# Moving the addition of the softmax's small constant from VectorE to GpSimd, one step ahead of the reciprocal

## The chip, the cores and the metric

The kernel runs on one core of a Trainium2 chip. The metric is the device time of one execution in microseconds (us). The kernel before takes 601.28 us, the median of three runs (601.18 to 601.39).

## What is computed

Banded attention with eight global keys, then two gated products. In the reference, cut to what matters here:

```python
def _attn_ref(q, k, v, n_global, n_local):
    ...
    scores = scale * np.matmul(q, k.transpose(0, 1, 3, 2))
    ...
    scores = scores + bias[None, :, :, :]
    scores = np.where(keep, scores, -1000000000.0)
    scores = scores - np.max(scores, axis=-1, keepdims=True)
    a = np.exp(scores)
    a = a / (np.sum(a, axis=-1, keepdims=True) + 1e-09)
    return np.matmul(a, v).astype(np.float32)
```

There are 2 batches, 8 heads, 768 positions and 64 numbers to a head; a query sees 96 keys up to its own and the first 8. What attention gives, 1536 x 512, goes through `(a * b) @ w3 @ w_out` with `a = x @ w1` and `b = x @ w2`, and then through a second product of that kind. The change touches the row sums of the softmax: the constant that is added to them, 1e-9, and the reciprocal that is taken of them.

## The kernel before

Attention works on tiles of 128 queries against 256 keys (their own 128 and the 128 before; the first tile of a batch sees 128). There are 12 tiles, and each has 4 units of two heads: 48 units `u`. `band_attention` is a software pipeline: each turn of its loop, called a step here, issues one stage each of several units, and since the instructions are put into the engines' queues in the order of the calls, and every queue is worked off in order, the order of the calls is the order on each engine. The next instruction of a queue waits until all that it needs is done, and holds those behind it.

In step `u`:

- TensorE gets the scores of units `u` and `u+1` in every second step (`band_scores`, L410 and L427).
- ScalarE gets the two exponentials of unit `u-2` (`band_exp`, L456), each of which also gives a row sum in one of the two columns of `z` (the rows with READ_ACCUMULATOR in the trace).
- `band_turn` transposes a unit four or five steps behind on TensorE (L480) and copies it on ScalarE (L482); `band_values` multiplies by the values (L516).
- VectorE gets `band_max` of unit `u-1`: two instructions L444, one for each head, which add the bias to the scores and find the row extreme.
- `band_norm` of unit `u-3`: VectorE adds the constant to `z` (L465), takes the reciprocal (L467), and GpSimd multiplies the exponentials by it, one instruction for each head (L469).
- In some steps the following come as well: splitting the next tile's keys and queries (ScalarE L368 and GpSimd L369 in one step, VectorE L380 and L383 in the next), the copy of the global keys L394, storing the result (ScalarE L491, VectorE L498), and the conversion of weights (ScalarE L89, L90, L115; VectorE L94, L98, L102, L119).

The stages written as generators are collected in `turns`, and `feed` takes them round robin: the first piece of each, then the second piece of each. So before the change VectorE's order in a step is: first L444, L465, the pieces of the other stages up to their first `yield`, second L444, L467, the rest. A stage without a `yield` (such as `band_high` with L369) runs at once when it is called, ahead of all pieces of the generators.

Between the steps, `next(filler)` puts matrix products of the next layer (`gate`, L669 to L671, with L677 on ScalarE and L678 on VectorE) into the queues. How much of it a step takes is counted in the code (`spent`) and doesn't depend on times.

Of the kernel before, what the change touches and what calls it, by code (L numbers as in the profile page):

```python
# [14 lines left out]
ALU = mybir.AluOpType  # L15
# [6 lines left out]
EPS = 1.0e-9  # L22
# [9 lines left out]
class Emitter:  # L32
# [418 lines left out]
    def band_exp(self, u):  # L451
# [7 lines left out]
            )  # L459
        self.sm[u] = (s, z, lo)  # L460

    def band_norm(self, u):
        nc = self.nc
        s, z, lo = self.sm[u]
        nc.vector.tensor_scalar_add(z, z, EPS)  # L465
        yield
        nc.vector.reciprocal(z, z)  # L467
        for j in range(2):
            nc.gpsimd.tensor_scalar(  # L469
                out=s[:, j, lo:], in0=s[:, j, lo:], scalar1=z[:, j : j + 1], scalar2=1.0, op0=ALU.mult, op1=ALU.mult  # L470
            )
# [51 lines left out]
    def band_attention(self, filler):  # L523

        self.v, self.qs, self.sp, self.sm, self.pt, self.pv = ({} for _ in range(6))
        self.kq = dict(enumerate(self.kq01))
        self.ks = self.const.tile([P, 3, self.H, P], F32R, name=self.name("ks"))
        self.globs = self.const.tile([P, self.H, MAX_GLOBAL], F32, name=self.name("globs"))
        C = self.C
        nt = self.B * self.NB  # L530
        nu = nt * C
        self.patient = True
        masks = self.band_masks()
        self.feed_load(1, self.nc.scalar)
        next(masks)

        self.nc.vector.tensor_copy(out=self.nf, in_=self.ni.bitcast(U32))
        next(masks)
        block_stages = (
            (0, self.band_load_v), (C - 1, self.band_global), (-3, self.band_low), (-4, self.band_high), (-6, self.band_load),  # L540
        )
        early = sorted((C * t + lag, t, n) for t in range(nt) for n, (lag, _) in enumerate(block_stages) if C * t + lag < 0)
        for _, t, n in early:
            if t and n != len(block_stages) - 1:
                for _ in block_stages[n][1](t) or ():
                    pass
        spent = 0.0
        turned = valued = 0
        stores = {}
        u = -1  # L550
        while self.stored < nt:
            u += 1
            self.step = u
            at = lambda lag, stage: stage(u - lag) if 0 <= u - lag < nu else None
            at(0, self.band_scores)
            at(2, self.band_exp)
            while turned < min(nu, u - 4 if u < 16 else u - 5):
                self.band_turn(turned)
                turned += 1


            while valued < min(nu, u - 5 if u < 16 else u - 6) and (u < self.pairs_from or u % 4 == 2):
                self.band_values(valued)
                valued += 1
                if valued % C == 0:
                    for n, stage in enumerate((self.store_x, self.store_x_low, self.set_stored)):
                        stores.setdefault(u + n, []).append((stage, valued // C - 1))
            turns = [at(1, self.band_max), at(3, self.band_norm)]
            turns += [stage(t) for stage, t in stores.pop(u, ())]
            for lag, stage in block_stages:  # L570
                t, c = divmod(u - lag, C)
                if c == 0 and 0 <= t < nt:
                    turns.append(stage(t))
            self.feed([x for x in turns if x])
            if u:
                next(masks, None)
            for _ in range(2):
                if spent < 0.85 * (u - 14) - 0.15 * max(u - 38, 0):
                    spent += next(filler)
        self.patient = False  # L580
# [918 lines left out]
```

## Time and profile before

| | us |
|---|---|
| median of three runs | 601.28 |
| the profiled execution | 600.37 |
| its span, first to last instruction | 598.5 |
| TensorE busy | 581.9 |
| VectorE busy | 446.2 |
| ScalarE busy | 366.3 |
| GpSimd busy | 171.3 |

The profiled execution is 600.37 us long, of which 598.5 us lie between the first and the last instruction. Busy times are of the whole span; an engine that is busy less than TensorE can still be the one that the others wait for in a part of it. In a timeline a row gives the start, the duration, the engine, the line, the operation and its tiles; what stands in brackets at its end is the idle time of the engine ahead of it and the instruction that ended it. PE is TensorE, DVE is VectorE, ACT is ScalarE, POOL is GpSimd.

### The profile page before, as it was taken

What the parts mean: (1) busy time and instruction counts of PE and PEld (TensorE: products, weight loads), DVE (VectorE), ACT (ScalarE), POOL (GpSimd) and SP (SyncE); (2) the same over time, 40 slices, a digit from 0 to 9 for tenths busy, and PEclk for the clock granted to TensorE, in tenths of its full rate; (3) what the DMA queues carried; (4) which work ended last, traced back from release to release, by engine and by line L of the source; (5) the groups of instructions that cost most, each with busy time, mean ns of one, the idle gap of its engine ahead of it and who ended that gap; (6) DMA issues with size and microseconds to landing.
All of it is one profiled execution on the core that took longest, in us unless ns stands there. A gap on an engine that the chain in (4) does not pass through costs nothing.

```text
span 598.5 us, 10290 instructions
## 1 busy us (share of the span) xinstructions
PE 581.9 (97%) x3632; PEld 507.8 (85%) x3632; DVE 446.2 (75%) x974; ACT 366.3 (61%) x802; POOL 171.3 (29%) x226
## 2 busy tenths in 40 slices
PE   6989999999999999999999999999999999999996
PEld 4678997888888888888899888888888888889996
DVE  6897989539967483739999777777777789984781
ACT  5998889747745473648664444444444465895830
POOL 5655767500000000422612022222222221555500
PEclk9999999999999999999999999999999999999999
DMA  8999683326424322796714012122220248999941
GB/s 231 283 250 239 161 214 104 113 72 208 140 71 142 124 88 70 141 231 126 109 28 141 34 54 79 47 70 71 72 71 2 71 136 220 235 143 191 195 99 57
DMA packets 31821, 76.78 MB, mean 128 GB/s; under 512 B 3601, under 2 KB 11281, under 8 KB 31761
## 3 DMA queue, kind: packets, MB, share of 16 engines
q1 hardware_dynamic: 20560, 57.42, 32.2%
q0 software_dynamic: 10624, 17.83, 18.0%
q10 hardware_dynamic: 576, 0.79, 0.5%
q8 instruction: 30, 0.49, 0.4%
q14 instruction: 31, 0.25, 0.1%
HBM read 55.05 MB, written 3.15 MB: 97 GB/s over the span
## 4 chain that ended last, share of the span: by engine, by line
PE 87%; DVE 6%; ACT 3%; issue 2%; POOL 1%; POOLq 0%; DVEq 0%; ACTq 0%
PE ab_band L931 29%; PE o_band L931 16%; PE y_band L931 10%; PE ab_band L669 7%; PE ab_band L670 6%; PE ab_band L671 6%; PE wfp_band L244 2%; PE wfp_band L243 2%; PE wfp_band L245 2%; PE pv_band L516 2%; DVE s_band L444 2%; PE pt_band L480 2%; ACT s_band L456 1%; DVE qb_band L383 1%; PE sp_band L410 1%
## 5 line engine op out<-in xcount | busy, mean ns | idle before, releaser
L931 PE MATMUL ab_band<-y_band,ws_band 128*128 128x512 f32 (+1 forms) x576 | 110.2, 337 | 0.0
L931 PEld LDWEIGHTS ab_band<-y_band,ws_band 128*128 128x128 f32 x576 | 91.1, 190 | 12.0
L669 PE MATMUL ab_band<-xh_band,w_band 128*128 128x512 f32 (+1 forms) x216 | 81.8, 379 | 0.0
L671 PE MATMUL ab_band<-xh_band,w_band 128*128 128x512 f32 (+1 forms) x216 | 79.1, 366 | 0.0
L670 PE MATMUL ab_band<-xl_band,w_band 128*128 128x512 f32 (+1 forms) x216 | 79.0, 366 | 0.0
L469 POOL TENSOR_SCALAR s_band<-s_band,z_band 128x256 f32<-128x256 f32 (+1 forms) x96 | 61.0, 648 | 35.9 <-DVE z_band L467 15.4
L931 PE MATMUL o_band<-wo_band,gs_band 128*128 128x256 f32 (+1 forms) x360 | 59.1, 326 | 0.0
L931 PE MATMUL y_band<-gs_band,wf_band 128*128 128x512 f32 (+1 forms) x336 | 58.4, 336 | 0.0
L931 PEld LDWEIGHTS o_band<-wo_band,gs_band 128*128 128x128 f32 x360 | 53.1, 190 | 5.9
L931 PEld LDWEIGHTS y_band<-gs_band,wf_band 128*128 128x128 f32 x336 | 51.8, 190 | 6.6
L931 PE MATMUL ab_band<-y_band,wa_band 128*128 128x512 f32 (+1 forms) x288 | 56.4, 338 | 0.0
L90 ACT ACTIVATE raw_band<-raw_band 128x512 int32<-128x512 uint32 x76 | 51.2, 674 | 0.0
L931 PEld LDWEIGHTS ab_band<-y_band,wa_band 128*128 128x128 f32 x288 | 46.0, 190 | 6.1
L678 DVE TENSOR_TENSOR g_band<-ab_band,b_band 128x512 f32<-128x512 f32 (+1 forms) x27 | 16.9, 629 | 45.2 <-ACT b_band L677 45.2
L456 ACT ACTIVATE s_band<-s_band,m_band 128x256 f32<-128x256 f32 (+1 forms) x96 | 46.8, 495 | 3.6 <-DVE m_band L444 3.4
L669 PEld LDWEIGHTS ab_band<-xh_band,w_band 128*128 128x128 f32 x216 | 40.7, 188 | 7.6 <-issue 1.0
L671 PEld LDWEIGHTS ab_band<-xh_band,w_band 128*128 128x128 f32 x216 | 40.6, 188 | 6.6
L670 PEld LDWEIGHTS ab_band<-xl_band,w_band 128*128 128x128 f32 x216 | 40.8, 189 | 6.1
L1133 ACT COPY p_band<-ab_band 128x512 f32<-128x512 f32 (+1 forms) x48 | 22.1, 484 | 33.2 <-PE ab_band L931 33.0
L799 POOL DMA_DIRECT2D wq_band<-wq_band x4 | 4.6, 1156 | 125.5 <-DVE wf_band L812 124.4
L1134 DVE TENSOR_TENSOR u_band<-ab_band,u_band 128x512 f32<-128x512 f32 (+1 forms) x24 | 13.3, 555 | 33.1 <-PE ab_band L931 32.6
L444 DVE CUSTOM_DVE_ANT_0 s_band<-sp_band,bias_band 128x256 f32<-128x256 f32 (+1 forms) x96 | 37.3, 391 | 0.6 <-ACT bias_band L309 0.4
(160 smaller groups left out, 1262.5 us busy)
## 6 DMA issues: line engine op xcount, KB each, us to landing
raw_band<-in_moe_w_dram SPq DMA_DIRECT2D x31, 512.0 KB, 4.8
raw_band<-in_moe_w_out_dram SPq DMA_DIRECT2D x20, 512.0 KB, 4.4
raw_band<-in_moe_w_b_dram SPq DMA_DIRECT2D x12, 512.0 KB, 3.5
raw_band<-in_moe_w_a_dram SPq DMA_DIRECT2D x12, 512.0 KB, 4.5
ga_band<-ga_band POOLq DMA_DIRECT2D x24, 256.0 KB, 6.8
v_band<-in_v_dram SPq DMA_DIRECT2D x12, 256.0 KB, 7.7
kd_band<-in_kq_dram SPq DMA_DIRECT2D x12, 256.0 KB, 6.6
qd_band<-in_kq_dram SPq DMA_DIRECT2D x12, 256.0 KB, 7.0
```

The lines of the kernel that those rows point to most:

```text
L90: nc.scalar.activation(out=low, in_=low.bitcast(U32), func=AF.Copy, scale=2.0**-29)
L243: nc.tensor.matmul(acc, w[:, 1, k % 4, :], o[:, 0, 0, :], start=(k == 0), stop=False)
L444: nc.vector.tensor_tensor_reduce(out=s[:, j, lo:], in0=sp[:, j, lo:], in1=bias[:, 2 * c + j, :], scale=-self.scale, scalar=FLT_MAX, op0=AL ...
L456: nc.scalar.activation(out=s[:, j, lo:], in_=s[:, j, lo:], func=AF.Exp, bias=m[:, j : j + 1], scale=-1.0, accum_out=z[:, j : j + 1],)
L469: nc.gpsimd.tensor_scalar(out=s[:, j, lo:], in0=s[:, j, lo:], scalar1=z[:, j : j + 1], scalar2=1.0, op0=ALU.mult, op1=ALU.mult)
L669: nc.tensor.matmul(p, wl, xh, start=(c == 0), stop=False)
L670: nc.tensor.matmul(p, wh, xl, start=False, stop=False)
L671: nc.tensor.matmul(p, wh, xh, start=False, stop=(c == self.C - 1))
L678: nc.vector.tensor_tensor(out=out[:, at], in0=ps[0], in1=b, op=ALU.mult)
L931: self.nc.tensor.matmul(bank, wt, xt, start=start and i == n == 0, stop=stop and n == 2 and i == len(terms) - 1, skip_group_check=more,)
L1133: copy = lambda out: nc.scalar.copy(out=out, in_=bank)
L1134: plus = lambda t: nc.vector.tensor_tensor(out=t, in0=bank, in1=t, op=ALU.add)
```

## The change

The addition is taken out of `band_norm` and becomes a stage of its own, `band_sum`, on GpSimd; it is issued for unit `u-2`, in the step in which that unit's exponentials are issued. With its `yield` gone `band_norm` is no generator any more: it runs when it is called, ahead of `band_max`, and its reciprocal comes first on VectorE in the step. On GpSimd the two multiplications of unit `u-3` come first, then the addition for unit `u-2`, and then what the other stages of the step issue there (L369).

```diff
+    def band_sum(self, u):
+
+        _, z, _ = self.sm[u]
+        self.nc.gpsimd.tensor_scalar(out=z, in0=z, scalar1=EPS, scalar2=1.0, op0=ALU.add, op1=ALU.mult)
+
     def band_norm(self, u):
         nc = self.nc
         s, z, lo = self.sm[u]
-        nc.vector.tensor_scalar_add(z, z, EPS)
-        yield
         nc.vector.reciprocal(z, z)
         for j in range(2):
             nc.gpsimd.tensor_scalar(
...
-            turns = [at(1, self.band_max), at(3, self.band_norm)]
+            at(3, self.band_norm)
+            at(2, self.band_sum)
+            turns = [at(1, self.band_max)]
```

## Rows read from the trace of the kernel before

**Rows 1.** The page: busy time by engine, and the chain's shares by engine.
```profile
PE 581.9 (97%) x3632; PEld 507.8 (85%) x3632; DVE 446.2 (75%) x974; ACT 366.3 (61%) x802; POOL 171.3 (29%) x226
...
PE 87%; DVE 6%; ACT 3%; issue 2%; POOL 1%; POOLq 0%; DVEq 0%; ACTq 0%
```

**Rows 2.** Line L465: durations (ns least/median/most), first and last start, waits ahead (us, times).
```profile
L465 DVE TENSOR_SCALAR z_band<-z_band x48: 156/166/822, 9.6 to 116.1; 128x2 f32<-128x2 f32 x48
...
  ACT s_band L456: 1.5, 2
```

**Rows 3.** Busy time of each engine by stretch, granted clock, DMA share, GB/s.
```profile
80.00:90.00 10.00, 10.00 (x76) 8.73 (x75) 9.91 (x35) 9.10 (x28) 6.50 (x9) 1.00 0.83 206
90.00:100.00 10.00, 8.64 (x77) 7.54 (x76) 9.80 (x31) 9.17 (x27) 7.46 (x9) 1.00 0.17 53
150.00:300.00 150.00, 150.00 (x663) 124.25 (x663) 105.43 (x156) 88.27 (x154) 22.65 (x24) 1.00 0.52 125
```

**Rows 4.** Timeline of TensorE: four of its eight idle gaps between 13 and 120 us.
```profile
33.03 0.66 PE L516 MATMUL pv_band<-pt_band,v_band 128*64 128x128 f32 x8 [0.75 <-ACT pt_band L482]
...
40.33 0.63 PE L480 MATMUL pt_band<-ident,s_band 128*128 128x128 f32 x4 [0.76 <-POOL s_band L469]
...
57.31 0.63 PE L480 MATMUL pt_band<-ident,s_band 128*128 128x128 f32 x4 [0.79 <-ACT pt_band L482]
...
94.08 0.39 PE L427 MATMUL sp_band<-ks_band,qb_band 128*128 128x256 f32 x1 [1.36 <-DVE ks_band L394]
```

**Rows 5.** Timeline of VectorE, 85 to 97 us.
```profile
85.36 0.41 DVE L444 CUSTOM_DVE_ANT_0 s_band<-sp_band,bias_band 128x256 f32<-128x256 f32 x1
...
86.19 0.40 DVE L444 CUSTOM_DVE_ANT_0 s_band<-sp_band,bias_band 128x256 f32<-128x256 f32 x1
...
86.52 0.78 DVE L465 TENSOR_SCALAR z_band<-z_band 128x2 f32<-128x2 f32 x1
87.34 1.47 DVE L380 TENSOR_TENSOR ks_band<-kd_band,ks_band 64x1024 fp32r<-64x1024 f32 x1
...
89.70 0.15 DVE L467 RECIPROCAL z_band<-z_band 128x2 f32<-128x2 f32 x1
...
92.92 0.41 DVE L444 CUSTOM_DVE_ANT_0 s_band<-sp_band,bias_band 128x256 f32<-128x256 f32 x1
...
93.26 0.17 DVE L465 TENSOR_SCALAR z_band<-z_band 128x2 f32<-128x2 f32 x1
93.33 0.42 DVE L444 CUSTOM_DVE_ANT_0 s_band<-sp_band,bias_band 128x256 f32<-128x256 f32 x1
...
93.67 0.16 DVE L467 RECIPROCAL z_band<-z_band 128x2 f32<-128x2 f32 x1
...
93.94 0.42 DVE L444 CUSTOM_DVE_ANT_0 s_band<-sp_band,bias_band 128x256 f32<-128x256 f32 x1
...
96.16 0.41 DVE L444 CUSTOM_DVE_ANT_0 s_band<-sp_band,bias_band 128x256 f32<-128x256 f32 x1
```

**Rows 6.** Group of L465: busy us, mean ns of one, idle before.
```profile
L465 DVE TENSOR_SCALAR z_band<-z_band 128x2 f32<-128x2 f32 x48 | 11.3, 234 | 1.5 <-ACT s_band L456 1.5
```

**Rows 7.** Timeline of GpSimd, 85 to 91 us.
```profile
85.31 0.93 POOL L469 TENSOR_SCALAR s_band<-s_band,z_band 128x256 f32<-128x256 f32 x2 [0.50 <-PE sp_band L427]
86.22 1.07 POOL L369 TENSOR_SCALAR qa_band<-qd_band 128x1024 fp32r<-128x1024 f32 x1
...
90.04 2.70 POOL L469 TENSOR_SCALAR s_band<-s_band,z_band 128x256 f32<-128x256 f32 x2 [0.88 <-PE pt_band L480]
```

**Rows 8.** GpSimd's instructions: line L469 (durations), and one memset's group (mean ns second).
```profile
L469 POOL TENSOR_SCALAR s_band<-s_band,z_band x96: 365/479/1821, 10.3 to 117.2; 128x256 f32<-128x256 f32 x80, 128x128 f32<-128x128 f32 x16
...
L1479 POOL MEMSET const-float32-1.0<- 128x1 f32 x1 | 0.1, 101 | 0.0
```

**Rows 9.** Timelines of GpSimd and VectorE, 4 to 5 us.
```profile
4.70 0.15 POOL L279 IOTA gl_band<- 128x32 f32 x1
...
4.86 0.29 DVE L286 TENSOR_SCALAR far_band<-rel_band 128x256 f32<-128x256 f32 x1 [3.98 <-POOL gl_band L279]
```

## The prediction

> **What bounds the kernel now.** I began with the page's busy shares and its chain [rows 1]: TensorE is busy for 97% of the span and carries 87% of the chain, VectorE 6%. All that the change touches lies in the attention stage, whose additions to the sums start between 9.6 and 116.1 us [rows 2]. After it TensorE is full: from 150 to 300 us it is busy for all 150.00 us [rows 3]. Since the change neither adds nor moves a TensorE instruction, the end can move only by the time in which TensorE stands idle before about 120 us. So I read next the stretches of 10 us [rows 3] and TensorE's idle gaps [rows 4]. From 80 to 90 us TensorE shows 10.00 of 10 and VectorE 9.91; from 90 to 100 us 8.64 and 9.80. The two run side by side, and where TensorE runs dry at 92.7 us it waits 1.36 us for VectorE's cast L394, an instruction of VectorE's step that begins at 92.92 [rows 4, 5]. So here a delay on VectorE is a delay of TensorE. The timeline of VectorE [rows 5] shows the rhythm: each step begins with the first of the two L444 (score plus bias, with the row minimum); the starts 85.36, 86.19, 92.92, 93.94 and 96.16 mark steps of 0.83, 6.73, 1.02 and 2.22 us, together 10.8 us for a tile. I call the first and third of them short; of the 48 steps 20 are under 1.5 us long, and these two stand for them.
>
> **What goes.** 48 additions (L465, median 166 ns) leave VectorE [rows 2]. The next instruction starts 0.07 us behind a usual one (93.26 to 93.33), so that is what one costs in the queue: 48 x 0.07 = 3.4 us. The summed duration is larger, 11.3 us, because some were held: the one at 86.52 took 0.78 us, while GpSimd ran the 1.07 us copy L369 until 87.29, and the longest took 0.82 [rows 2, 5 to 7]. I count nothing for these: L380 right behind it started 0.05 us after the copy ended, has two inputs in SBUF, and needs what the addition was waiting for. The Trainium skill (SBUF — State Buffer, Terms) says that VectorE and GpSimd share a port pair by an exclusive lock held for a whole instruction, the loser blocking fully; the trace agrees with it at 86.52. By that rule taken alone the change looks like a gift, since it takes away 48 requests for the lock; it is weighed as a rival below.
>
> **What comes on GpSimd.** 48 additions of 128x2. No row shows one. Upper bound: of GpSimd's 96 multiplications, tensor_scalar too, the shortest, with 128 columns, takes 365 ns, and the median, with 256, 479 ns [rows 8]; the line through the two falls to 0.25 us at two columns. Lower bound: its memset of 128x1 takes 0.10 us [rows 8], and less than nothing is excluded, for an instruction is added to an in-order queue. I take 0.25, since it is the same operation; 0.10 and 0.25 stay as ends. GpSimd is busy for 29% of the span [rows 1], so the 12 us by themselves cost nothing. What they cost is in the order.
>
> **What moves, and the new wait.** In the new order a step u issues on GpSimd: the two multiplications L469 of unit u-3, the addition for unit u-2, then the copy L369 in every fourth step (before, that copy came ahead of the multiplications). On VectorE the reciprocal of u-3 comes first, ahead of both L444. It now waits for GpSimd's addition, issued in the step before behind the multiplications of u-4, and these wait for the reciprocal that opened that step. Queued behind the waiting reciprocal stands all of VectorE's step: L444 (for which ScalarE's exponentials wait), L380, L394, L383 (for which the scores wait) and the weight conversion. Before, VectorE waited for ScalarE alone at this place: twice, 1.5 us in all [rows 2]; GpSimd could lag by a step without VectorE noticing.
>
> So every step gets a least length, the round trip: from the start of a reciprocal to the start of its multiplications 0.34 us (89.70 and 90.04 [rows 5, 7]), the pair 0.93 (85.31 [rows 7]), the addition 0.25, and the way back to VectorE. That way is 0.01 to 0.02 us where VectorE waited longest for GpSimd, 4.85 to 4.86 [rows 9]; I take 0.05, with 0.02 and 0.15 as ends. The sum is 0.34+0.93+0.25+0.05 = 1.57 us, with ends of 1.39 and 1.67.
>
> **Steps against the round trip, 85 to 103 us.** A short step is now 0.83-0.07 = 0.76 or 1.02-0.07 = 0.95 us of VectorE work, and becomes 1.57: it grows by 0.74 or by 0.55. The step of 2.22 stays longer than the round trip and loses its addition: -0.07. The long step begins with a wait for the copy: before, L380 started 1.15 us after the step's start (86.19 to 87.34); after, the copy begins when the addition ends, about when VectorE's reciprocal starts, and lasts 1.07, so L380 starts 1.05 to 1.15 after it: -0.05. A tile of four steps therefore grows by 0.74-0.05+0.55-0.07 = 1.17 us (a round trip of 1.39 gives 0.8, one of 1.67 gives 1.4). The 20 us from 80 to 100, in which both engines are full or TensorE waits for VectorE [rows 3], hold two such tiles: 2 x 1.17 = 2.3 us (1.6 to 2.8) by which TensorE's gaps grow, as it has none of its own to spare there.
>
> **Steps before 80 us.** Here the picture is mixed. TensorE's gaps end at 33.03 us (0.75) and 57.31 us (0.79) behind ScalarE's copy L482 and at 40.33 us (0.76) behind GpSimd's multiplications; with the one at 94.08 they are four of the eight over 0.2 us between 13 and 120 us, and two more, ending at 24.98 and 62.48, are behind L482 too [rows 4]. The reciprocal goes earlier in its step by both L444 and all between them, at least 0.75 us (92.92 against 93.67 [rows 5]), so the multiplications start earlier; that can take away the gap at 40.33 and shorten that at 57.31: -0.8 to -1.5 us. Against this stand short steps just ahead of 33, 40, 57 and 62 us, each longer by 0.55 to 0.74. Four of them are 2.6 us, and part is covered by VectorE's own idle time there. I take +2.3 for the delays that arrive and -1.2 for the gaps that close: +1.1 us, between -1.5 and +2.6.
>
> **The sum.** 2.3 + 1.1 = +3.4 us. The profiled execution took 600.37 us, of which 598.5 are span and 1.9 lie around it; 600.37 + 3.4 = 603.8, and the median of the runs, 601.28, lies 0.91 above that execution: 604.7 us. With the low ends -1.5+1.6 = +0.1, with the high ones +2.6+2.8 = +5.4.
>
> **Rivals.** First, hidden: the round trip is real but VectorE's delays end before they reach TensorE, because the earlier multiplications give back in each tile what the wait takes. For it: TensorE has only a handful of gaps. Against it: the gap at 92.7 us waits for VectorE itself, not for GpSimd. It gives 601.28 within 1.2 us.
>
> Second, faster: the addition on GpSimd is cheap (0.10) and the way back 0.02, VectorE gets back its 3.4 us and also the time in which its additions were held, (234-166) ns x 48 = 3.3 us from mean and median [rows 2, 6], and the gaps at 40.33 and 57.31 close. Taken on the chain, that is 0.15 us in each of the 2.5 tiles after 79 us, 0.4 us, some 0.7 of the held additions there, and 1.5 us of gaps: 601.28-2.6 = 598.7. It decides where steps are longer than the round trip, that is if VectorE's short steps lie in cover. For it: TensorE waited for GpSimd's products at the gap of 40.33. Against it: 20 short steps. The lock of the Trainium skill (SBUF — State Buffer, Terms) is the mechanism by which this rival's held additions are given back; the trace shows the holding at 86.52, and also L380 held by the same copy.
>
> Third, worse by starvation: in long steps the multiplications are themselves held by VectorE's instructions with two SBUF inputs (the pair at 90.04 took 2.70 us instead of 0.93 [rows 7]), and an addition behind them that is not through when the long step ends adds up to its pair's 0.5 to 0.9 us in each of the 12 tiles. It decides if the pair, now started at the head of the step, is still open when the step ends. That is +6 us on top of half of the sum: 609 us. Against it: a long step has 6 us, and the pair that now starts earliest has only one other behind it. That the reciprocal would not come first in the queue after all I count with the hidden case: it is called before the generator of L444 is advanced.
>
> **How the numbers follow.** The forecast 604.7 (+1.2 to +6) gets 0.52, hidden 0.24, faster 0.15, starvation 0.09. About 0.2%, 1.2 us, is what a measurement of this kernel can tell from no change. So slower has 0.52+0.09 = 0.61, same 0.24, faster 0.15. The range of 8 in 10 leaves out about half of the faster case and most of starvation: 600.0 to 608.5. It is wider upwards than the ends of the sum, because the step lengths were walked for two tiles of twelve.
>
> **What would show it.** In the profile after: the reciprocals preceded by idle time of VectorE that ends on GpSimd's addition, some 20 times by 0.5 to 0.8 us, hardly any in long steps; the additions between 0.1 and 0.3 us when not held; starts of L444 in short steps at least 1.4 us apart; TensorE's gap at about 93 us grown from 1.36 to over 2 us; the gap at 40 us gone. If the idle time of VectorE before the reciprocals sums to less than 5 us, or TensorE's gaps before 120 us sum to no more than now, the prediction is wrong in its main step; if the way back from GpSimd takes over 0.2 us, or long steps wait too, it is too low.

## The result, and the profile after

The changed kernel takes 607.33 us (median of five runs, 606.85 to 607.78), beside 601.28 us for the kernel before in the same comparison (600.46 to 601.64). The ratio is 1.0108, with a 95% interval of 1.0097 to 1.0119: slower by 6.05 us. Forecast were +3.4 us. The direction and the range held; the size was too small by a factor of 1.8. The profiled execution of the changed kernel took 606.85 us, 605.0 of them span, against 600.37 and 598.5 before; so the two traces compared below differ by 6.5 us.

In the new code the addition on GpSimd is line L465, the reciprocal L470, the multiplications L472, the transposes L483 with their copies L485, and the values L519. Lines up to L456 have kept their numbers.

The page, busy time by engine and the chain's shares (before: [rows 1]):

```profile
PE 583.6 (96%) x3632; PEld 509.7 (84%) x3632; DVE 442.2 (73%) x926; ACT 367.9 (61%) x802; POOL 178.2 (29%) x274
...
PE 86%; ACT 4%; POOL 3%; DVE 2%; issue 2%; DMA 1%; ACTq 1%; POOLq 0%; DVEq 0%
```

VectorE is relieved as planned, 4.0 us less busy and 48 instructions fewer; its share of the chain falls from 6% to 2%. GpSimd gains 6.9 us of work, and its share of the chain rises from 1% to 3%. None of this tells that the kernel is slower. That is read from what the two moved lines wait for.

The reciprocal and the addition by line: durations (ns least/median/most), first and last start, and under them what ended the idle time of the engine ahead of them (us, times):

```profile
L470 DVE RECIPROCAL z_band<-z_band x48: 148/165/168, 9.2 to 123.3; 128x2 f32<-128x2 f32 x48
...
  POOL z_band L465: 16.6, 23
```

```profile
L465 POOL TENSOR_SCALAR z_band<-z_band x48: 191/192/1219, 8.8 to 123.1; 128x2 f32<-128x2 f32 x48
...
  ACT s_band L456: 2.7, 5
```

Before, VectorE waited 1.5 us, twice, at the addition [rows 2]. Now it waits 16.6 us, 23 times, at the reciprocal, and for GpSimd's addition each time.

The timeline of VectorE from 97.7 to 100 us (its L444 accumulator reads left out), one short step:

```profile
97.74 0.15 DVE L470 RECIPROCAL z_band<-z_band 128x2 f32<-128x2 f32 x1
97.82 0.40 DVE L444 CUSTOM_DVE_ANT_0 s_band<-sp_band,bias_band 128x256 f32<-128x256 f32 x1
...
99.31 0.17 DVE L470 RECIPROCAL z_band<-z_band 128x2 f32<-128x2 f32 x1 [0.73 <-POOL z_band L465]
99.39 0.27 DVE L394 CAST ks_band<-globs_band 128x256 fp32r<-128x256 f32 x1
```

and GpSimd in the same stretch:

```profile
98.07 0.93 POOL L472 TENSOR_SCALAR s_band<-s_band,z_band 128x256 f32<-128x256 f32 x2 [2.58 <-DVE z_band L470]
99.08 0.19 POOL L465 TENSOR_SCALAR z_band<-z_band 128x2 f32<-128x2 f32 x1
```

This is the round trip. The reciprocal starts at 97.74, the multiplications it releases at 98.07, the addition behind them at 99.08, and the next reciprocal, which waited for that addition, at 99.31: 1.57 us. VectorE's own work in the step was over 0.73 us earlier. Worked out from the starts of all 48 reciprocals, 15 of the 47 steps are between 1.56 and 1.58 us long and four are shorter (1.34 and 1.49 us); a length that repeats to a hundredth is that of a loop, not of the work in it.

The timeline of TensorE: the gaps that answer to [rows 4], that at 65.43, and those at 18.93, 75.04 and 88.39 that were not there before:

```profile
18.93 0.80 PE L410 MATMUL sp_band<-kq,kq_band 64*128 64x128 f32 x4 [2.82 <-DVE kq L394]
...
35.34 0.66 PE L519 MATMUL pv_band<-pt_band,v_band 128*64 128x128 f32 x8 [0.70 <-ACT pt_band L485]
42.61 0.63 PE L483 MATMUL pt_band<-ident,s_band 128*128 128x128 f32 x4 [0.73 <-POOL s_band L472]
...
59.74 0.63 PE L483 MATMUL pt_band<-ident,s_band 128*128 128x128 f32 x4 [0.79 <-ACT pt_band L485]
...
65.43 2.02 PE L519 MATMUL pv_band<-pt_band,v_band 128*64 128x128 f32 x32 [0.99 <-ACT pt_band L485]
...
75.04 2.02 PE L519 MATMUL pv_band<-pt_band,v_band 128*64 128x128 f32 x32 [0.37 <-ACT pt_band L485]
...
88.39 0.39 PE L427 MATMUL sp_band<-ks_band,qb_band 128*128 128x256 f32 x1 [0.79 <-DVE ks_band L394]
99.72 0.39 PE L427 MATMUL sp_band<-ks_band,qb_band 128*128 128x256 f32 x1 [2.53 <-DVE ks_band L394]
```

Since TensorE's instructions and their order are the same in both kernels, the same instruction can be looked up in both traces, and the difference of its starts tells how much has been lost by then:

| start before, us | start after, us | lost so far, us |
|---|---|---|
| 16.70 (scores L410) | 18.93 | 2.23 |
| 24.98 | 27.28 | 2.30 |
| 33.03 | 35.34 | 2.31 |
| 40.33 | 42.61 | 2.28 |
| 57.31 | 59.74 | 2.43 |
| 62.48 | 65.43 | 2.95 |
| 71.65 | 75.04 | 3.39 |
| 83.94 | 88.39 | 4.45 |
| 94.08 | 99.72 | 5.64 |
| 106.17 | 112.77 | 6.60 |

So the loss has two places: 2.2 us in one piece before 19 us, then 0.2 in all up to 57 us, and 4.2 us in small pieces, about 1 us for each tile, from there to the end of the stage. The spans differ by 6.5, so nothing is lost behind it. TensorE's gaps of over 0.2 us between 13 and 120 us sum to 11.1 us, to 5.9 before; and the same instructions keep it busy for 1.7 us longer (583.6 against 581.9 [rows 1]).

The piece before 19 us, on GpSimd's timeline of the changed kernel (L321 makes the bias tables that the first steps need):

```profile
15.35 0.19 POOL L465 TENSOR_SCALAR z_band<-z_band 128x2 f32<-128x2 f32 x1
15.62 1.31 POOL L321 TENSOR_SCALAR bias_band<-dist_band 128x256 bf16<-128x256 f32 x2
17.03 0.72 POOL L472 TENSOR_SCALAR s_band<-s_band,z_band 128x128 f32<-128x128 f32 x2
17.84 0.19 POOL L465 TENSOR_SCALAR z_band<-z_band 128x2 f32<-128x2 f32 x1
```

and on VectorE's:

```profile
15.57 0.17 DVE L470 RECIPROCAL z_band<-z_band 128x2 f32<-128x2 f32 x1 [0.99 <-POOL z_band L465]
...
18.06 0.17 DVE L470 RECIPROCAL z_band<-z_band 128x2 f32<-128x2 f32 x1 [1.05 <-POOL z_band L465]
18.61 0.27 DVE L394 COPY kq<-globs_band 128x128 f32<-128x128 f32 x1 [0.39 <-issue]
```

Here the trip is 2.49 us long, because the tables L321 stand in GpSimd's queue between the addition and the next multiplications. Two such waits, one of 0.99 us at 10.95, and 0.39 us ahead of the copy itself for which the profile shows no reason put off VectorE's copy L394, for which TensorE's scores wait at 18.93. Before, the same copy began at 14.99 and the scores came without a gap.

Stretches of the changed kernel: busy PE, PEld, DVE, ACT, POOL, then the granted clock, DMA share, GB/s:

```profile
10.00:20.00 10.00, 6.85 (x46) 4.72 (x46) 6.36 (x27) 7.99 (x27) 8.48 (x21) 0.91 1.05 299
...
20.00:22.00 2.00, 2.00 (x16) 1.29 (x14) 1.86 (x7) 0.86 (x4) 0.51 (x2) 0.50 1.08 347
...
98.00:100.00 2.00, 0.28 (x2) 0.28 (x3) 1.27 (x9) 1.40 (x5) 1.48 (x4) 1.00 0.01 4
100.00:102.00 2.00, 2.00 (x13) 2.00 (x12) 2.00 (x8) 1.21 (x5) 1.07 (x3) 0.54 0.00 0
102.00:104.00 2.00, 2.00 (x8) 1.63 (x7) 1.08 (x8) 1.70 (x4) 1.81 (x4) 0.60 0.00 0
```

Between 10 and 20 us all three engines of the chain are less busy than before (before: PE 9.64, DVE 9.08, POOL 9.41 us of 10): they wait for each other in turn. After the gap of 2.53 us the granted clock shows 0.54 and 0.60, for most of the time the lower of its two levels (1.2 GHz). Whether that is a part of the 6 us is asked in experiments 11 and 12. It is 0.50 from 20 to 24 us as well, behind the gap of 2.82 us; before, it was 1.00 from 21 us on. There TensorE's delay rose from 2.23 us to 3.06 (at the start that was at 23.64 before) and fell back to 2.30, because the gap of 0.69 us that ended at 24.98 before is gone. What this stretch would have cost at the full clock no run shows.

### The profile page after: what moved, and what is told of

Read it like the earlier page. It is cut to its first block, busy times and chain, and to the rows that moved or that the text cites. A ratio compares the mean times of both kernels' runs of the same rounds, so it can differ in the third digit from the quotient of the medians.

```text
span 605.0 us, 10310 instructions
## 1 busy us (share of the span) xinstructions
PE 583.6 (96%) x3632; PEld 509.7 (84%) x3632; DVE 442.2 (73%) x926; ACT 367.9 (61%) x802; POOL 178.2 (29%) x274
## 4 chain that ended last, share of the span: by engine, by line
PE 86%; ACT 4%; POOL 3%; DVE 2%; issue 2%; DMA 1%; ACTq 1%; POOLq 0%; DVEq 0%
PE ab_band L936 29%; PE o_band L936 15%; PE y_band L936 10%; PE ab_band L674 7%; PE ab_band L675 7%; PE ab_band L676 7%; PE wfp_band L243 2%; PE wfp_band L245 2%; PE wfp_band L244 2%; PE pv_band L519 2%; PE pt_band L483 2%; POOL s_band L472 2%; ACT s_band L456 2%; PE sp_band L427 1%; ACT pt_band L485 1%
## 5 line engine op out<-in xcount | busy, mean ns | idle before, releaser
L472 POOL TENSOR_SCALAR s_band<-s_band,z_band 128x256 f32<-128x256 f32 (+1 forms) x96 | 53.0, 564 | 29.8 <-DVE z_band L470 21.4
L456 ACT ACTIVATE s_band<-s_band,m_band 128x256 f32<-128x256 f32 (+1 forms) x96 | 46.5, 489 | 8.5 <-DVE m_band L444 7.8
L771 POOL TENSOR_TENSOR sf_band<-gb_band 128x256 f32<-128x256 f32 x12 | 10.3, 861 | 95.3 <-DVE gb_band L102 76.4
```

The costliest lines, as they stand in the source:

```text
L456: nc.scalar.activation(out=s[:, j, lo:], in_=s[:, j, lo:], func=AF.Exp, bias=m[:, j : j + 1], scale=-1.0, accum_out=z[:, j : j + 1],)
L472: nc.gpsimd.tensor_scalar(out=s[:, j, lo:], in0=s[:, j, lo:], scalar1=z[:, j : j + 1], scalar2=1.0, op0=ALU.mult, op1=ALU.mult)
```

## The experiments

My theory was that the round trip costs the time: VectorE's reciprocal waits for GpSimd's addition, which stands behind multiplications that wait for the reciprocal before. The rivals: the place (the reciprocal ahead of both L444 puts off the exponentials), the load (48 more instructions on GpSimd), and, after the ledger above, the bias tables in the trip and TensorE's clock. Edits are against the changed kernel if nothing else is said. Each result stands beside runs of the kernel before on the same chip; "difference" is from their median.

| kernel | us | before, us | difference | ratio [95%] |
|---|---|---|---|---|
| changed | 607.33 | 601.28 | +6.05 | 1.0108 [1.0097, 1.0119] |
| 1 no addition | 599.26 | 601.02 | -1.76 | 0.9973 [0.9964, 0.9983] |
| 2 addition back on VectorE, first | 604.57 | 601.02 | +3.55 | 1.0065 [1.0041, 1.0089] |
| 3 on GpSimd, reciprocal late | 603.35 | 601.02 | +2.33 | 1.0043 [1.0025, 1.0061] |
| 4 on GpSimd, result unread | 601.97 | 601.02 | +0.95 | 1.0015 [1.0003, 1.0027] |
| 5 only from unit 12 on | 603.31 | 600.92 | +2.39 | 1.0045 [1.0027, 1.0062] |
| 6 addition ahead of the pair | 605.06 | 600.92 | +4.14 | 1.0071 [1.0053, 1.0089] |
| 7 two additions | 610.36 | 600.53 | +9.83 | 1.0160 [1.0143, 1.0177] |
| 8 before, without the addition | 598.52 | 600.92 | -2.40 | 0.9968 [0.9955, 0.9980] |
| 9 on GpSimd, needs and feeds nothing | 601.05 | 600.92 | +0.13 | 1.0009 [0.9996, 1.0022] |
| 10 tables on ScalarE | 606.41 | 600.53 | +5.88 | 1.0093 [1.0077, 1.0110] |
| 11 18 products in TensorE's gap | 607.20 | 600.53 | +6.67 | 1.0108 [1.0091, 1.0125] |
| 12 8 products there | 608.05 | 600.08 | +7.97 | 1.0132 [1.0115, 1.0149] |

**1. No addition; the reciprocal stays first.**

```diff
             at(3, self.band_norm)
-            at(2, self.band_sum)
             turns = [at(1, self.band_max)]
```

> The reciprocal stays first in VectorE's step, and the addition of 1e-9 is left out altogether. Three theories of the 6 us by which the changed kernel (607.33) is slower than the one before (601.28). Wait: the reciprocal waits for GpSimd's addition, which stands behind the pair of multiplications. Place: the reciprocal at the head of the step holds the step back whatever it waits for (it now waits for ScalarE ahead of both L444). Load: GpSimd has 48 more instructions, which take its time and the port that it shares with VectorE. The wait theory expects 598.5 to 601 us, since 48 additions at 0.07 us in VectorE's queue are gone and nothing is put in their place; load expects the same; place expects 605 to 607.

599.26 us, ratio 0.9973. With the reciprocal in the new place and nothing to wait for, the kernel is faster than before. The place alone is not what costs 6 us. Load, too, had been expected to give this.

**2. The addition back on VectorE, directly ahead of the reciprocal, both first in the step.**

```diff
+        nc.vector.tensor_scalar_add(z, z, EPS)
         nc.vector.reciprocal(z, z)
...
-            at(2, self.band_sum)
```

> The addition goes back to VectorE, directly ahead of the reciprocal, both at the head of the step; GpSimd's order is that of the changed kernel without the addition. Wait and load: 600 to 602 us, with no waits for GpSimd ahead of these two. Place: 605 to 607, since only the waiting engine differs.

604.57 us lies between what the two theories wanted, and neither explains it. VectorE's timeline of this kernel:

```profile
96.50 0.16 DVE L470 TENSOR_SCALAR z_band<-z_band 128x2 f32<-128x2 f32 x1
96.69 0.17 DVE L471 RECIPROCAL z_band<-z_band 128x2 f32<-128x2 f32 x1
96.78 0.40 DVE L444 CUSTOM_DVE_ANT_0 s_band<-sp_band,bias_band 128x256 f32<-128x256 f32 x1
```

The reciprocal, which needs the addition's result, starts 0.19 us behind it, and L444, which needs nothing of either, 0.09 behind the reciprocal: 0.28 us for the two. In the kernel before the second L444 stood between them, and an addition held the queue for 0.07 us [rows 5]. With 0.08 for a reciprocal (97.74 to 97.82) that makes 0.15, so the pair costs some 0.13 us more in each of 48 steps, 6.2 us on VectorE. That this makes the 3.55 us is not shown. TensorE's starts in this trace put most of the loss elsewhere: 1.3 us ahead of the kernel before at the start that was at 23.64 there, it is 2.1 us behind at the one that was at 33.03, and 4.4 at the end of the stage. In between stand a wait for ScalarE's copy,

```profile
24.87 0.91 PE L520 MATMUL pv_band<-pt_band,v_band 128*64 128x128 f32 x8 [1.88 <-ACT pt_band L486]
```

and a granted clock of 0.50 from 26 to 32 us. Against experiment 1 the addition at the head of the step costs 5.3 us, as much as the wait does in experiment 4: work of VectorE put there delays this kernel as well as a wait. So this run does not measure the place by itself, as it was meant to; experiment 1 does.

**3. Addition on GpSimd, the reciprocal back behind both L444.** `band_norm` is a generator again, and `band_sum` becomes one, so that the copy L369 stands ahead of the multiplications on GpSimd, as before the change.

```diff
+        yield
         nc.vector.reciprocal(z, z)
...
+            turns = [at(1, self.band_max), at(3, self.band_norm), at(2, self.band_sum)]
```

> The addition stays on GpSimd, behind the pair of multiplications, but the reciprocal goes back to its old place behind both L444 of the step (and the copy L369 ahead of the pair). The round trip now has at least 0.75 us more before VectorE needs the sum, but the pair starts that much later too, so the trip itself is as long. Wait: the trip of reciprocal, pair, addition and reciprocal is a loop that does not depend on the place in the step; a short step still lasts at least about 1.5 us, and the time stays at 605 to 608; what changes is that both L444 come ahead of the stall, so that ScalarE's exponentials start in time, which may give back 1 to 3 us. Place: 601 to 602. Load: 606 to 608.

603.35 us: 3.7 us less than the changed kernel by the differences, more than was expected. What VectorE waits for ahead of the reciprocal here (us, times):

```profile
  POOL z_band L466: 12.3, 26
```

The waits fall only from 16.6 to 12.3 us. But now they stand behind both L444, and the exponentials wait less for these. What ScalarE waits for L444 (us, times), first in the changed kernel, then in this one:

```profile
  ACT s_band L456: 7.8, 12
```

```profile
  ACT s_band L456: 3.9, 7
```

Both kernels have GpSimd's addition and VectorE's wait for it; what differs is who stands behind the waiting instruction, and where the copy L369 stands. How much each of the two gives back was not separated.

**4. The addition on GpSimd writes into a spare tile that nobody reads.** The reciprocal is taken of the sums themselves, into a tile `r` of its own.

```diff
+        spare = self.small.tile([P, 2], F32, tag="spare", name=self.name("spare"))
-        self.nc.gpsimd.tensor_scalar(out=z, in0=z, ...
+        self.nc.gpsimd.tensor_scalar(out=spare, in0=z, ...
...
+        nc.vector.reciprocal(r, z)
```

> GpSimd makes the same 48 additions at the same places, but into a spare tile that nothing reads; the reciprocal reads the sums without the constant and writes to a tile of its own, so it waits for ScalarE alone. The constant's addition is thereby left out of the result. Wait: 599 to 601.5 us, the additions hidden. Load: 606 to 608. Place: 605 to 608.

601.97 us, half a microsecond above what the wait had been expected to leave. The same 48 instructions in the same place, after the same exponentials, and only VectorE's wait for them is gone (its trace, of the longest of the ten executions, 604.25 us, has none): 5.1 us of the 6.05 go with it. This is the experiment that shows that the wait is the cost. The two intervals are far apart.

**5. The addition only for units 12 to 47.**

```diff
     def band_sum(self, u):
+        if u < 12:
+            return
```

> GpSimd adds the constant for units 12 to 47 only; for units 0 to 11 it is left out, and their reciprocals wait for ScalarE alone. Between the changed kernel (607.33 us) and the one without any addition (599.26) lie 8.1 us. In the trace of the changed kernel TensorE is 2.3 us behind the kernel before at 25 us, in that without addition 1.5 us ahead of it: 3.8 us of the 8.1 arise in the first units, where GpSimd also writes the bias tables. If that is so: 603.5 us, within 1. If the wait costs the same in every unit, 12 of 48 units hold 2.0 us: 605.3. If the first units' delay is made up later anyway: 607.

603.31 us, 3.7 us less. The scores of TensorE's timeline that began at 16.70 before and at 18.93 in the changed kernel come here without a gap at

```profile
15.84 0.80 PE L410 MATMUL sp_band<-kq,kq_band 64*128 64x128 f32 x4
```

That is 3.1 us earlier than in the changed kernel: the 2.2 us that it lost before 19 us, and 0.9 because these units have no addition on either engine. So the piece ahead of 19 us comes from the first units' additions. How much of it reaches the end this trace doesn't tell: it is of the longest of the four executions (605.03 us; the others took 603.11 to 603.37), and at the end of the stage 1.7 of the 3.1 us are left.

**6. GpSimd's addition ahead of the multiplications.** The addition then stands ahead of the pair of its step, and a trip through one pair spans two steps.

```diff
-            at(3, self.band_norm)
             at(2, self.band_sum)
+            at(3, self.band_norm)
```

> As the changed kernel, but GpSimd gets the addition of unit u-2 ahead of the pair of multiplications of unit u-3. The reciprocal's wait then spans two steps for one pair, so the round trip no longer sets a least length of a step; in its place the pair waits behind an addition that waits for the exponentials of its own step. If the round trip through the pair is what costs: 601 to 604 us, with under half of the 16.6 us of VectorE's waits for the addition. If it is the load on GpSimd or the place of the reciprocal: 606 to 608. A cost of the new kind, the pair late for the transposes, shows as waits of TensorE for L472 and lies within the first range.

605.06 us, less was given back than expected: 1.9 us. What GpSimd waits for ahead of the addition, and what VectorE waits for ahead of the reciprocal:

```profile
  ACT s_band L456: 16.1, 18
```

```profile
  POOL z_band L465: 6.4, 11
```

VectorE's waits fall from 16.6 to 6.4 us as the theory said, but a new wait takes their place: GpSimd now waits 16.1 us for ScalarE's exponentials of unit `u-2`, and the multiplications of unit `u-3`, which could run, are queued behind.

**7. Two additions of half the constant each.** This lengthens the suspected trip by one addition, and doubles the 48 instructions on GpSimd.

```diff
-        self.nc.gpsimd.tensor_scalar(out=z, in0=z, scalar1=EPS, ...
+        for _ in range(2):
+            self.nc.gpsimd.tensor_scalar(out=z, in0=z, scalar1=EPS / 2, ...
```

> As the changed kernel, but GpSimd adds half of the constant twice, one addition behind the other. Each round trip is longer by a second addition, 0.19 us by its median and perhaps 0.1 more since it reads what the first wrote. If the round trip sets the short steps, the waits of VectorE for the addition grow from 0.73 to about 0.95 us where they now show 0.73, 23 x 0.2 = 4.6 us in all, of which TensorE gets about a third (it got 6.1 us from 16.6): 608.5 to 611. If the waits have another cause, such as the port: 607 to 608.

610.36 us, 3.8 us more than the changed kernel. VectorE's waits, and a reciprocal of its timeline:

```profile
  POOL z_band L466: 22.6, 27
```

```profile
60.92 0.17 DVE L471 RECIPROCAL z_band<-z_band 128x2 f32<-128x2 f32 x1 [0.91 <-POOL z_band L466]
```

A wait that was 0.73 us is 0.91: the trip is longer by one addition, 0.18 us. For the 19 steps that the changed kernel has at or under 1.58 us this is 3.4 us; 3.8 were measured. A loop that sets the step length behaves like this. The load alone is not excluded for a part of it: 48 additions without any dependence cost 1.9 us in experiment 9.

**8. The kernel before, without its addition.**

```diff
-        nc.vector.tensor_scalar_add(z, z, EPS)
         yield
         nc.vector.reciprocal(z, z)
```

> The kernel before without the addition of the constant, the reciprocal in its old place behind both L444. It splits the 1.8 us by which the kernel without addition and with the reciprocal first (599.26) is faster than the one before (601.02 beside it). If the 48 additions in VectorE's queue make it, this one takes 599.0 to 599.8. If the earlier reciprocal makes it, through earlier multiplications, 600.7 to 601.3.

598.52 us, below both ranges, ratio 0.9968: the 48 additions in VectorE's queue are worth 2.4 us. No run that moves them brought more. Experiment 1 differs from this one by the place of the reciprocal and its multiplications (there ahead of the copy L369, here behind it) and has -1.76; the intervals overlap, so the earlier place brings nothing that can be seen. This version is faster than both kernels. It leaves out the constant; each row's extreme is taken off before the exponential, so that a sum holds exp(0) = 1 and is at least about 1, and in float32 1e-9 added to such a number leaves it as it is.

**9. The same addition on GpSimd, of a table that is long ready, into the spare tile.** It doesn't wait for the exponentials, and nothing needs its result.

```diff
-        self.nc.gpsimd.tensor_scalar(out=z, in0=z, ...
+        self.nc.gpsimd.tensor_scalar(out=spare, in0=self.nf[:, 0:2], ...
```

> As the kernel with the unread addition (601.97 us), but the addition reads a table that is ready from the start, so that it never waits for ScalarE's exponentials; the constant is not added to the sums. The unread addition cost 2.7 us against no addition (599.26). Waiting: GpSimd's addition, waiting for the exponentials of its unit (8 times, 6.7 us in that trace), holds what stands behind it, above all the copy L369 and the bias tables; then this kernel takes 599.3 to 600.3. Load: its time and the port are the cost; then it stays at 601.5 to 602.5.

601.05 us, between the two ranges that were expected. By line:

```profile
L465 POOL TENSOR_SCALAR spare_band<-nf x48: 192/193/1217, 8.4 to 116.9; 128x2 f32<-128x2 f32 x48
```

Against experiment 1, which differs by these instructions alone, this is 1.9 us more, and the intervals don't overlap: 9 us of tiny instructions on an engine that is busy for 29% of the span cost 1.9 us. Against experiment 4 it is 0.8 us less, the price of the addition's own wait for ScalarE, if it is one: here the intervals overlap. In the two traces TensorE is 0.8 us later than in experiment 1 by 19 us, where GpSimd is full, still 0.8 at 90 us and 1.7 at the end of the stage. Of the ten runs the five with a mean granted clock of 0.997 and above took 600.08 to 601.09 us, the five below 601.00 to 602.43, so that some of the 1.9 us goes with the clock. How they divide between that, the queue and the time in which additions and VectorE's instructions hold each other up was not separated.

**10. The bias tables L321 on ScalarE.** This takes them out of the trip of the first steps.

```diff
-            nc.gpsimd.tensor_scalar(
-                out=self.bias[:, h, :], in0=dist, scalar1=factor, ...
+            nc.scalar.mul(self.bias[:, h, :], dist, factor)
```

> As the changed kernel, but the eight bias tables L321 are written by ScalarE instead of GpSimd. In the changed kernel's trace two of them (0.77 us) stand between a reciprocal and its multiplications in each of the steps of 10 to 18 us, so there the round trip is 1.8 to 2.5 us instead of 1.57. If these tables in the trip make the loss of the first units (4.0 us by the run that adds from unit 12 on), up to 4 x 0.77 = 3.1 us come back, less what ScalarE loses with eight instructions of about 0.3 us while it is busy for 8 of 10 us: 604.5 to 606.5. If the first units lose by the wait itself, tables or not: 607 to 608.

606.41 us, the difference from before 0.2 us less than the changed kernel's by medians and 0.9 by the ratio; the intervals overlap, so no gain is shown. TensorE's timeline ahead of the same scores (here line L408), where the changed kernel has a gap of 2.82 us:

```profile
16.87 0.70 PE L517 MATMUL pv_band<-pt_band,v_band 128*64 128x128 f32 x4 [1.07 <-ACT pt_band L483]
17.75 0.80 PE L408 MATMUL sp_band<-kq,kq_band 64*128 64x128 f32 x4 [0.18 <-DVE kq L392]
```

The place answers as the reading of the trace wanted: the scores start 1.2 us earlier. But TensorE has a gap of 1.07 us behind ScalarE just before, and what is gained there is spent further on: the lead of 1.2 us is 0.7 behind a wait of 1.23 us for ScalarE's copy at 41.92 (0.73 at 42.61 in the changed kernel), and 0.4 at the scores that begin at 99.35 (99.72), for which VectorE's cast sets the time. That the tables in the trip make the larger part of the gap is borne out; that they make 2.2 us of the end is not.

**11 and 12. Identity products in TensorE's gap near 98 us,** 18 and, in the second kernel, 8, ahead of the scores of unit 40 (the trace has two records for each). If the half clock behind the gap is a term of the sum, a gap that is filled gives it back.

```diff
+        if u == 40:
+            for _ in range(18):
+                nc.tensor.matmul(sp[0][:, 0, :P], self.ident, self.ident, start=True, stop=True)
```

> As the changed kernel, but TensorE gets 18 more products of the identity with itself, into a bank that the scores of unit 40 overwrite, just ahead of those scores: where the trace shows it idle for 2.53 us, before the granted clock stands at 0.5 for 3.4 us from 100.25 us. They depend on nothing that is late. If the half clock follows from the idle time and costs what the trace shows there, 1.4 us: 605.6 to 606.4, the clock at 1.00 from 95 to 110 us. If the half clock comes whatever TensorE does there, or costs nothing since VectorE sets the pace: 607.0 to 607.8.

> As the run with the filled gap, with 8 products instead of 18. There the 18 took 4.18 us, 1.5 us more than the idle time that they filled, and the clock stayed at 1.00: what the clock gave back the products took. Eight take 8/18 of 4.18 = 1.9 us and end within the 2.53 us. If the half clock after the gap costs 1.4 us of the changed kernel's time: 605.6 to 606.4, with the clock at 1.00 from 95 to 110 us. If the half clock only changes its place, or VectorE sets the pace there: 607.0 to 607.8.

With 18 the products themselves took 4.18 us, longer than the gap, and the time of 607.20 says little. The 8 fit it, on TensorE's timeline of that kernel:

```profile
97.16 1.95 PE L407 MATMUL sp_band<-ident 128*128 128x128 f32 x16
99.86 0.39 PE L430 MATMUL sp_band<-ks_band,qb_band 128*128 128x256 f32 x1 [0.76 <-DVE ks_band L394]
...
111.12 0.36 PE L430 MATMUL sp_band<-ks_band,qb_band 128*128 128x256 f32 x1 [1.06 <-DVE ks_band L394]
```

and its stretch of 100 to 102 us:

```profile
100.00:102.00 2.00, 2.00 (x15) 1.92 (x16) 2.00 (x9) 1.21 (x4) 1.23 (x3) 1.00 0.00 0
```

The clock stays at 1.00 where the changed kernel had 0.54. The time does not fall: 608.05 us, above both ranges, and a span of 605.3 against 605.0. TensorE works faster and then waits 1.06 us at 111.12, for the next cast on VectorE, where the changed kernel came to its scores without a gap. That cast comes no earlier; first in the changed kernel, then in this one:

```profile
110.53 0.27 DVE L394 CAST ks_band<-globs_band 128x256 fp32r<-128x256 f32 x1
```

```profile
110.70 0.27 DVE L394 CAST ks_band<-globs_band 128x256 fp32r<-128x256 f32 x1
```

What paces this tile is VectorE's steps; a slower TensorE only used up time in which it would have waited. So the half clock near 100 us is an effect of the change and no part of its cost that can be seen. The runs of experiment 7 agree: at mean granted clocks of 0.986, 0.986, 0.995 and 0.996 they took 610.25, 610.49, 610.42 and 610.29 us. The half clock from 20 to 24 us was not taken away in any run.

## Why the prediction was right, and where it fell short

**The bound.** Right. All of the loss lies in the attention stage, most of it as growth of TensorE's gaps; the gap at 93 us, for which over 2 us was forecast, is 2.53 us. TensorE waits there and at 88.39 for VectorE; the gaps at 65.43 and 75.04 wait for ScalarE's copy.

**The round trip.** Right, to the hundredth, though not by each of its parts. Measured at 97.74 to 99.31: 0.33 to the multiplications, 0.93 for the pair, 0.08 until the addition starts, 0.19 for it, 0.04 for the way back. The addition was put too high from GpSimd's larger instructions (0.25, measured 0.192 as a median), and the 0.08 between the pair's end and the addition was left out. That the two cancel to the hundredth is luck.

**VectorE's waits.** Right: "some 20 times by 0.5 to 0.8 us" was forecast, and 23 waits of 0.72 us on the average came, 16 of them between 0.5 and 0.8. Starts of L444 at least 1.4 us apart were forecast for short steps; two steps, of a tile whose multiplications have 128 columns only, are 1.34.

**Two tiles at 80 to 100 us.** Right: +2.3 us by the sum; the ledger shows 1.06 (71.65 to 83.94) and 1.19 (83.94 to 94.08), together 2.25. VectorE's steps bear out the terms: the reciprocals from 86.38 to 97.74 are 1.58, 1.64, 1.56 and 6.58 us apart, where the steps before (82.77 to 92.92) were 1.02, 1.57, 0.83 and 6.73; the tile grew by 1.21, and 1.17 was forecast. In the next one, +0.96, the short steps grew as forecast, but the third step grew by 0.2 and the long one shrank by 0.5.

**What of the tiles was not counted.** The stretch that the prediction walked ended at 100 us, while the additions went on to 116 [rows 2]. The last tile lost about the same again, 0.96 us (94.08 to 106.17), with no gap longer than 0.2 us to show for it: TensorE was at half clock for a part of it, was 7.2 us late for a while, and came to its next scores, at 111.31, half a microsecond after VectorE's cast at 110.53 was done. This is the first failed step. The page's view of a stretch in which the bound engine is full does not tell that it is held up.

**Steps before 80 us.** This is the step that failed most. +1.1 us was taken, the balance of +2.3 for delays that arrive and -1.2 for gaps that close; up to 71.65 us, +3.4 was measured. Both halves of the balance were wrong in their place. Neither gap closed: the one at 40.33 us was to go, and is 0.73 us at 42.61 (0.76 before), and the one at 57.31 is 0.79 us as before. The trip is not the reason. In experiment 1, where the reciprocal comes first and waits for no addition, both are still there, behind ScalarE's copy:

```profile
39.21 0.63 PE L483 MATMUL pt_band<-ident,s_band 128*128 128x128 f32 x4 [0.77 <-ACT pt_band L485]
...
56.35 0.63 PE L483 MATMUL pt_band<-ident,s_band 128*128 128x128 f32 x4 [0.79 <-ACT pt_band L485]
```

So earlier multiplications don't shorten these gaps, and the -1.2 us had no ground. (The gap that did go, at 24.98, was no gain: it took up a delay.) And the delays came elsewhere: 2.2 us in one piece before 19 us, where I had walked no step. There GpSimd was busy for 9.41 of 10 us before, with the bias tables; the trip went round through them and was 2.5 us long, not 1.57. I had costed one trip, with GpSimd otherwise idle, and applied it to a stretch in which GpSimd was full. Between 19 and 57 us, where I had put three of the four delays, 0.2 us was lost in all.

**"GpSimd is busy for 29%, so the 12 us by themselves cost nothing."** Wrong. Experiment 9 against experiment 1 gives 1.9 us for the same instructions without any dependence. The 29% are over the whole span; in the attention stage GpSimd is busy for over 80 of the first 130 us of the changed kernel. How much of the 1.9 us is in the changed kernel beside the trip isn't known, since the two were measured in different kernels.

**The gain on VectorE.** 48 x 0.07 = 3.4 us was an upper bound of it; experiment 8 measures 2.4 us at the end.

**The parts together,** by the differences of the table: additions out of VectorE's queue -2.4 (8), reciprocal first +0.6 (1 against 8, not separated from zero), 48 instructions on GpSimd +1.9 (9 against 1), their wait for ScalarE +0.8 (4 against 9, not separated from zero), the reciprocal's wait for them +5.1 (the changed kernel against 4). These add up to +6.05 because they are steps of one row; each carries the uncertainty of two ratios, some 1 us, and what the granted clock made of either kernel.

**The rivals.** Hidden and faster are out. The starvation rival had the wrong steps: none of the 11 steps of over 3 us ends in a wait. On GpSimd's timeline around 95 us the addition of the long step:

```profile
94.39 1.10 POOL L465 TENSOR_SCALAR z_band<-z_band 128x2 f32<-128x2 f32 x1
```

It was held while VectorE's L383 ran (94.22 to 95.43), and was through 2.2 us before the reciprocal at 97.74 that needed it. The exclusive lock that the Trainium skill (SBUF — State Buffer, Terms) describes agrees with this row, 1.10 us in place of 0.19; but held in a long step, the addition costs VectorE no wait. The lock was the mechanism of the faster rival, as the way to give held time back. It did not decide the case.

**Open.** Why VectorE's steps in experiment 10 give up a lead of over 1 us by 99 us; how the 1.9 us of GpSimd's load come about; why an addition at the head of VectorE's step costs as much as the wait (experiment 2); what the half clock from 20 to 24 us cost; and whether the trip through the tables would cost 2.2 us at the end if the later tiles were not paced by the same loop.

## What to carry to other kernels

When an operation is moved from one engine's queue to another's and its result comes back, follow the loop: if each engine's next step waits for the other's last, the sum of hand-overs and of all that is queued in between is a least length for every step, however idle the engines are on the average. Cost that loop in each stretch with what the other queue holds there, and walk every stretch in which the operation occurs, the crowded first steps above all. A wait may be better put behind the work that others wait for than ahead of it: moving the reciprocal back behind L444 (and the copy L369 with it) gave back over half of the loss though VectorE still waited 12.3 us in place of 16.6.

## What was not expected of the hardware

- Two VectorE instructions of 128x2 of which the second needs the first take 0.28 us of the queue (0.19 + 0.09); with an independent instruction between them such an addition took 0.07 (experiment 2, [rows 5]).
- GpSimd's 128x2 addition has a median of 0.192 us, and as much when it depends on nothing (0.193). From its 128- and 256-column instructions [rows 8] 0.25 was worked out.
- The hand-over from GpSimd to VectorE took 0.04 us (99.08 + 0.19 to 99.31); that from VectorE to GpSimd 0.33 us from start to start (97.74 to 98.07), 0.18 from the reciprocal's end. The price of the loop is in the work, not in the way.
- A TensorE gap of 2.53 us was followed by the half level of the clock, and one that was filled with products was not; the time of the kernel did not fall by it (608.05 and 607.33 us), as VectorE's cast came no earlier.
